# Attention and a gated feed-forward layer in one kernel: idle matrix products in the opening, edge loads on ScalarE's queue, additions for a reduction, and a table of priorities for the planned order

## The chip, the cores and the metric

The kernel runs on one core of a Trainium2 chip. The metric is the device time of one execution in microseconds (us). A time of "before" is the median of three runs; the profile is of one further execution, whose own time differs a little from that median and is given beside it below. Engines are called as in the profile: PE (TensorE, matrix products; PEld are its weight loads), DVE (VectorE), ACT (ScalarE), POOL (GpSimd) and SP (SyncE, which only issues transfers here). ACT and POOL issue transfers too.

## What is computed

The reference, cut to what matters:

```
B, H, S, D = 8, 8, 576, 64;  factor = 4
q_d, k_d, v_d = means of q, k, v over groups of 4 positions        # 144 rows
out_d  = softmax(q_d k_d^T / 8) v_d,  repeated 4 times along S     # coarse attention
local  = softmax(q k^T / 8, only |i - j| < 4) v                    # a band of 7 keys
x      = out_d + local, as 4608 rows of 512
xn     = x / sqrt(mean(x^2) + 1e-6) * rms_g
out    = (silu(xn w_gate) * (xn w_val)) w_out                      # 512 -> 1536 -> 512
```

## The kernel before

**The work.** The 4608 rows go through the feed-forward layer (`Forward`) in 18 chunks of 256. For each chunk, and for each of the 12 blocks of 128 hidden columns (f = 0 to 11), PE makes a gate part and a value part (line 1259, 12 products of 128x256 each) and, one pair of blocks later, the second layer (line 1296, 6 products of 128x512 each). Each fp32 operand is split into a high and a low part, so that three products of the fast type replace one of full precision: `xh`, `xl` for the rows, two tiles for each weight. The twelve blocks use three groups of weights, f = 0 to 3, 4 to 7 and 8 to 11.

**What must come before a chunk.** Chunk 0 and chunk 1 get their rows from `Early`: band attention on PE for two units of 128 rows each (units 0 and 1 for chunk 0, units 2 and 3 for chunk 1). A unit has four `score` steps (lines 1048 and 1050: a mask product of `one_sb` with `near_sb`, then the keys against `q`), maxima on DVE (line 1063), exponentials on ACT (line 1074), transposes (line 1108), the products with the values (line 1133), and the addition of the coarse result with a spreading matrix (line 1139). All other chunks get their rows from `Attention`, which works on DVE and ACT. The coarse attention (`Coarse`, lines 498, 526 and 540 on PE) comes in 32 items; the four of batch 0 belong to the opening, and their sums over four positions are made in the kernel by `OpeningSums`: `load_qk` fetches four parts, `add` (line 406) sums them on DVE with one reduction for each half, and `order` (line 402) copies the queries of the half to a tile `hs` on ACT, from which `score` takes them.

**The edges.** `Early.load_values` loads the 128 value rows of a unit (line 1028), and then, with eight small transfers of 2 KB (line 1036), the rows on its two sides into a tile of the pool `kv`, which POOL has cleared. Four units make 32 of these, and all are issued by SP.

**The weights.** They come as 64-bit words and are decoded in 20 pieces: the raw words are fetched by SP (line 249) into one of a few raw places, then POOL (line 264), ACT (line 254), DVE (line 271), ACT (line 278) and DVE (lines 283 and 285) make the high and the low tile. A raw place is free for the next piece when the last of these steps is done.

**What sets the order.** For the opening (all of the work until the third chunk is under way), a planner (`Plan`) writes the order of every engine by hand. Each `task` has an engine, a cost, a due time and what it waits for; the planner runs its own clock, and among the tasks that could start on an engine at about the same time takes the one with the smallest due time. Every engine executes its list in that order. After the opening, a loop writes the chunks in turn, and a scheduler sets the order.

A transfer from SP or ACT raises one of eight semaphores, given out in turn over both queues in the order in which the planner writes the transfers; an instruction that issues a transfer first waits until the transfer that had its semaphore before has landed.

Of the kernel before, what the change touches and what calls it, by code (L numbers as in the profile page):

```python
# [8 lines left out]
FP32 = mybir.dt.float32  # L9
# [5 lines left out]
ALU = mybir.AluOpType  # L15
# [23 lines left out]
EDGE = 2 * FAC  # L39
SPREAD = 13 * GRP  # L40
# [6 lines left out]
ON_TENSOR = 2  # L47
# [3 lines left out]
NEAR = 0.15  # L51
MB = 3.1
LAND = 2.0
ISSUE = 0.9

# [19 lines left out]
class Plan:  # L75


    def __init__(self, bufs):
        self.tasks, self.bufs = [], bufs
        self.order = {r: [] for r in bufs}  # L80
# [47 lines left out]
    def run(self, until=1e9):  # L128
        free, ready = self.free, self.ready
        while self.left:  # L130
            best = None
            for e, tasks in ready.items():
                found = []
                for t in tasks:
                    at = self.room(t) if t.allocs else 0.0
                    if at is not None:
                        floor = free["DMA"] - 3.0 if t.dma else 0.0
                        found.append((max(free[e], t.at, at, floor), t))
                if not found:
                    continue  # L140
                first = min(s for s, _ in found)
                pick = min(
                    ((next(o for o in t.options if o[0] == e)[2], t.n, s, t) for s, t in found if s <= first + NEAR),
                    key=lambda x: x[:2],
                )
                if best is None or pick[2] < best[0]:
                    best = (pick[2], e, pick[3])
            assert best, [t.fn for tasks in ready.values() for t in tasks][:40]
            s, e, t = best
# [3 lines left out]
            t.start = s  # L153
            free[e] = s + cost
# [19 lines left out]
def attn_moe_kernel(  # L174
# [34 lines left out]
    near_sb = const.tile([P, FAC * (NEAR_K + 1)], BF16, name="near_sb")  # L209

# [156 lines left out]
    class OpeningSums:  # L367


        def __init__(self, b, half):  # L370
# [5 lines left out]
            add = task("DVE", 2.5, self.add, at, [self.got], allocs=[self.qk_buf])  # L376
            self.q_got = task("ACT", 1.1, self.order, at - 1, [self.got], allocs=[self.q_buf])
# [26 lines left out]
        def add(self):  # L404
            self.qk = glob.tile([P, 2, 2, SD], FP32, name="qk")
            nc.vector.tensor_reduce(
                out=self.qk.rearrange("p t h n -> p (t h n)"),
                in_=self.raw_qk.rearrange("p j x -> p x j"), axis=AX.X, op=ALU.add,
            )

        def add_v(self, j, engine):
            if j == 1:
# [3 lines left out]
                out=vs, in0=self.raw_v[:, 0] if j == 1 else vs, in1=self.raw_v[:, j], op=ALU.add,  # L416
            )
# [3 lines left out]
    class Coarse:  # L421
# [28 lines left out]
        def plan(self, at, after=()):  # L450
# [12 lines left out]
            scores = task("PE", 0.75, self.scores, at, [*sm.ready_qk, *after], allocs=[*s, m, z], uses=[sm.qk_buf])  # L463
# [5 lines left out]
            for par in range(2):  # L469
                exps.append(task(  # L470
                    "ACT", 0.45, lambda par=par: self.powers(par), at, [scale], allocs=[a[par]], uses=[s[par], m, z],
                ))
            for par in range(2):
                turn = task("PE", 0.6, lambda par=par: self.turn(par), at - TAIL, [exps[par]], allocs=[t[par]], uses=[a[par]])
# [4 lines left out]
            values = self.valued = task("PE", 1.3, self.values, at - TAIL, [*copies, *sm.ready_vs], allocs=[o], uses=[*a, sm.vs_buf])  # L479
# [6 lines left out]
            stored[b, hp] = task("ACT", 0.06, self.store, at, [scaled], uses=[og], lag=2.2)  # L486
            return self

        def scores(self):
# [3 lines left out]
            self.s = [self.pool.tile([HALF, 2, SD], FP32, name=self.tag) for _ in range(2)]  # L493
            qs, ks = self.sums.qk[:, 0], self.sums.qk[:, 1]
# [27 lines left out]
        def turn(self, par):  # L522
            tp = self.t[par] = self.pool.tile([HALF, 2, SD], FP32, name=self.tag)
            for kc in range(2):
# [10 lines left out]
        def values(self):  # L535
            op = self.o = self.pool.tile([HALF, 2, 2, D], FP32, name=self.tag)
            for par, at in enumerate(self.a):
# [102 lines left out]
    class Attention:  # L640
# [55 lines left out]
        def plan(self, newton="POOL"):  # L696
# [7 lines left out]
            for n, jp in enumerate(jps):  # L704
                k_bufs[jp] = buf("kv"), buf("q_t")
                loaded[jp] = task(
                    "SP", 0.15, lambda jp=jp: self.load_score(*jp), T - 88 + 7 * n, allocs=k_bufs[jp],
# [20 lines left out]
            for n, jp in enumerate(jps):  # L728
                v_bufs[jp] = buf("kv")
                v_loaded[jp] = task(  # L730
                    "SP", 0.1, lambda jp=jp: self.load_value(*jp), T - 55 + 7 * n, allocs=[v_bufs[jp]],
# [774 lines left out]
```

## Time and profile before

| | |
|---|---|
| median of three runs | 1131.25 us (1128.24 to 1132.88) |
| profiled execution: its own time | 1137.31 us |
| profiled execution: span from first to last instruction | 1135.5 us |
| mean granted TensorE clock | 0.989 |
| PE busy, share of the span | 1083.9 us, 95% |
| DVE / ACT / POOL busy | 79% / 53% / 13% |
| lines 1259 and 1296, share of the chain that ended last | 50% and 25% |

How to read the lines below. A row of windows has the stretch in us, its length, then for PE, PEld, DVE, ACT and POOL the busy time with the count of instructions in brackets, the granted TensorE clock (1.00 is full speed), the busy share of the DMA engines, and GB/s. A row of the timeline has the start in us, the length, the engine, the line, the operation with out<-in, the shape and the count (a row merges equal neighbours); in square brackets stands how long the engine was idle before, and what ended that. SPq, ACTq and POOLq are the issuing of transfers. A row of waits has who waited for whom, the sum in us, how many times, and the longest.

### The profile page before, as it was taken

The numbers are of one execution on the slowest core, as the hardware profiler recorded it, in microseconds if no ns is written. First come the engines' busy times: TensorE is split into PE (matmuls) and PEld (weight loads), VectorE is DVE, ScalarE is ACT, GpSimd is POOL, SyncE is SP. The second block draws the span as 40 slices with busy tenths as digits, with TensorE's granted clock in tenths as the row PEclk, the third lists the DMA queues.
The fourth block names the chain that finished last, engine by engine and source line by source line (L and its number), as shares of the span: only waits on it lengthen the run. The fifth ranks groups of instructions, "written<-read, shape, count | busy, mean of one in ns | idle before, by whom it ended". The sixth has DMA issues, their size and how long they took to land.

```text
span 1135.5 us, 21446 instructions
## 1 busy us (share of the span) xinstructions
PE 1083.9 (95%) x7878; PEld 987.3 (87%) x7878; DVE 900.8 (79%) x1519; ACT 597.8 (53%) x2033; POOL 142.2 (13%) x178
## 2 busy tenths in 40 slices
PE   4699969989999999999999999999999999999997
PEld 3567869869999999999999999999999999999997
DVE  5365987869997979797979797979797989887321
ACT  3465547455646555555555555555555473736111
POOL 4242313332111010101010101010000000000000
PEclk9999989989999999999999999999999999999999
DMA  6755644636264344434343435343131313220000
GB/s 161 272 209 142 179 121 110 127 85 151 67 154 91 109 95 120 85 109 94 109 96 105 99 95 109 103 102 98 43 99 43 103 45 101 69 58 19 1 20 19
DMA packets 79619, 114.07 MB, mean 100 GB/s; under 512 B 32666, under 2 KB 41114, under 8 KB 79514
## 3 DMA queue, kind: packets, MB, share of 16 engines
q1 hardware_dynamic: 50026, 89.52, 25.8%
q0 software_dynamic: 10080, 18.59, 10.5%
q10 hardware_dynamic: 19408, 4.60, 1.9%
q8 instruction: 62, 1.02, 0.4%
q14 instruction: 43, 0.35, 0.1%
HBM read 100.86 MB, written 11.80 MB: 99 GB/s over the span
## 4 chain that ended last, share of the span: by engine, by line
PE 88%; DMA 5%; DVE 2%; ACT 2%; SPq 1%; issue 1%; POOL 0%; ACTq 0%; DVEq 0%; POOLq 0%
PE ps_h L1259 50%; PE ps_o L1296 25%; PE ps_a L540 3%; PE ps_a L498 2%; PE ps_a L526 2%; PE ps_a L926 1%; DMA wo<-in_w_val_dram 1%; PE ps_o L1133 1%; SPq L1036 1%; PE ps_h L1050 1%; DMA w<-in_v_pad_dram 1%; DMA w<-in_v_sum_dram 1%; PE ps_a L1133 1%; DMA q_t<-in_q_band_dram 1%; PE ps_a L1108 0%
## 5 line engine op out<-in xcount | busy, mean ns | idle before, releaser
L1259 PE MATMUL ps_h<-xh,w 128*128 128x256 f32 x3456 | 635.5, 281 | 10.7 <-ACT w L278 6.4
L1259 PEld LDWEIGHTS ps_h<-xh,w 128*128 128x128 f32 x3456 | 540.3, 189 | 22.7 <-ACT w L278 6.8
L1259 PE MATMUL ps_h<-xl,w 128*128 128x256 f32 x1728 | 483.5, 280 | 0.0
L1296 PE MATMUL ps_o<-wo,hs 128*128 128x512 f32 x1296 | 333.5, 399 | 1.7 <-POOL hs L1283 1.6
L1259 PEld LDWEIGHTS ps_h<-xl,w 128*128 128x128 f32 x1728 | 327.2, 189 | 6.5 <-issue 1.7
L857 ACT ACTIVATE prod<-kv,sc 128x64 f32<-128x64 f32 x1024 | 263.7, 407 | 30.4 <-DVE sc L848 19.8
L1296 PEld LDWEIGHTS ps_o<-wo,hs 128*128 128x128 f32 x1296 | 233.4, 189 | 46.4 <-POOL hs L1283 2.7
L874 DVE TENSOR_REDUCE x_t<-prod 128x128 f32<-128x896 f32 x128 | 135.0, 1078 | 47.4 <-PE ps_a L926 41.3
L1266 ACT ACTIVATE sil<-ps_h 128x512 f32<-128x512 f32 x108 | 64.5, 597 | 168.3 <-PE ps_h L1259 159.7
L1280 ACT ACTIVATE hs<-sil 128x512 fp32r<-128x512 f32 x108 | 68.2, 631 | 155.0 <-DVE sil L1274 134.2
L811 DVE TENSOR_TENSOR prod<-q_t,kv 128x896 f32<-128x896 f32 x128 | 140.0, 1099 | 0.5
L815 DVE TENSOR_REDUCE sc<-prod 128x14 f32<-128x896 f32 x128 | 136.7, 1076 | 0.5
L1269 DVE SCALAR_TENSOR_TENSOR sil<-sil,ps_h 128x512 f32<-128x512 f32 x108 | 73.5, 681 | 50.1 <-ACT sil L1266 49.8
L864 DVE TENSOR_TENSOR prod<-sc,kv 128x384 f32<-128x384 f32 (+1 forms) x128 | 103.6, 865 | 0.2
L1274 DVE SCALAR_TENSOR_TENSOR sil<-sil,ps_h 128x512 f32<-128x512 f32 x108 | 74.4, 690 | 30.5 <-PE ps_h L1259 30.3
L356 POOL DMA_DIRECT2D qk<-in_qk_sum_dram x42 | 37.7, 899 | 419.1 <-DMA qk<-in_qk_sum_dram 320.2
L1283 DVE TENSOR_TENSOR hs<-sil,hs 128x512 fp32r<-128x512 f32 x100 | 68.7, 687 | 18.9 <-ACT hs L1280 18.7
L897 ACT ACTIVATE up_t<-x_t 128x128 f32<-128x128 f32 x128 | 39.3, 307 | 44.0 <-DVE x_t L887 39.3
L517 ACT ACTIVATE a_g<-ps_a,m_g 72x144 f32<-72x144 f32 x128 | 46.4, 370 | 15.1 <-DVE m_e L1067 8.3
L605 ACT COPY a_g<-ps_a 72x288 f32<-72x288 f32 x63 | 22.8, 400 | 45.5 <-PE ps_a L526 45.3
L356 POOL DMA_DIRECT2D vs<-in_v_sum_dram x42 | 38.5, 916 | 53.3 <-DMA vs<-in_v_sum_dram 46.4
L540 PEld LDWEIGHTS ps_a<-vs,a_g 72*72 72x72 f32 x512 | 41.8, 159 | 1.3 <-ACT w L1074 0.5
(142 smaller groups left out, 806.9 us busy)
## 6 DMA issues: line engine op xcount, KB each, us to landing
kv<-in_k_pad_dram SPq DMA_DIRECT2D x56, 320.0 KB
kv<-in_v_pad_dram SPq DMA_DIRECT2D x56, 320.0 KB
qk<-in_qk_sum_dram POOLq DMA_DIRECT2D x42, 288.0 KB, 4.5
out_dram<-o_sb SPq DMA_DIRECT2D x96, 72.0 KB
q_t<-in_q_band_dram SPq DMA_DIRECT2D x170, 36.0 KB
vs<-in_v_sum_dram POOLq DMA_DIRECT2D x42, 144.0 KB, 4.4
w<-in_w_gate_dram SPq DMA_DIRECT2D x8, 512.0 KB
w<-in_w_val_dram SPq DMA_DIRECT2D x8, 512.0 KB
```

What stands on the lines that cost most here:

```text
L356: nc.gpsimd.dma_start(out=t, in_=(qk_sum, v_sum)[i][self.b, j, :, self.half], accum_op=ALU.add)
L540: nc.tensor.matmul(out=op[:, par, c], lhsT=at[:, kc, c * HALF:(c + 1) * HALF], rhs=self.sums.vs[:, 2 * (self.hp % 2) + par, kc], start=(kc ...
L811: nc.vector.tensor_tensor(out=pr, in0=bcast(q[:, s0:s0 + 2], 2, NO), in1=window(k, s0), op=ALU.mult)
L815: nc.vector.tensor_reduce(out=self.sc[:, j, par, s0:s0 + 2], in_=self.pr[i], axis=AX.X, op=ALU.add,)
L857: nc.scalar.activation(out=self.pr[i][:, o, s], in_=self.v[j, par][:, s0 + s + o], func=AF.Copy, scale=p[:, s, o:o + 1],)
L864: (nc.vector if engine == "DVE" else nc.gpsimd).tensor_tensor(out=self.pr[i][:, a:b], in0=bcast(p[:, :, a:b].rearrange("p s o -> p o s"), ...
L874: nc.vector.tensor_reduce(out=self.x[j][:, s0:s0 + 2, par], in_=pr.rearrange("p o s d -> p s d o"), axis=AX.X, op=ALU.add,)
L1259: nc.tensor.matmul(out=p[n][:, i], lhsT=wi[:, k], rhs=xi[:, k], start=(m == 0), stop=(m == 3 * KT - 1),)
L1269: nc.vector.scalar_tensor_tensor(out=self.sil[n], in0=self.sil[n], scalar=1.0, in1=self.g[n], op0=ALU.add, op1=ALU.mult,)
L1274: nc.vector.scalar_tensor_tensor(out=self.sil[n], in0=self.sil[n], scalar=0.5, in1=self.v[n], op0=ALU.mult, op1=ALU.mult,)
L1283: (nc.gpsimd if engine == "POOL" else nc.vector).tensor_tensor(out=self.hs[n][:, 1], in0=self.sil[n], in1=self.hs[n][:, 0], op=ALU.subtract,)
L1296: nc.tensor.matmul(out=self.o[j], lhsT=lhs[:, cols], rhs=rhs, start=(f == 0 and m == 0), stop=(f == NF - 1 and m == 2),)
```

## The change

- **Idle products.** A new function `heat` is called at the head of most PE steps of the opening. Where the planner's clock has PE idle ahead of the step, it writes products of a tile `zero_sb` (zeros in bf16) with `one_sb` into the output tile of the step, before the step's own products: 0.75 of the planned idle time, if that share is over 0.6 us. In the built program there are 60 of them: 35 of 256 columns ahead of the first `score`, 8 and 5 of 256 ahead of two transposes of the first coarse item, 8 of 512 ahead of the first product of chunk 0, and 4 of 512 in its second layer.
- **Edges.** The 32 small transfers become a task of their own, `load_edges`, issued by ACT. `load_values` keeps the one transfer of a unit.
- **Sums.** `add` becomes three additions for each half in place of one reduction.
- **Order.** A table `RANK` of one number for each task replaces the due times in the planner's choice (the diff shows its first line), and many costs are set anew.
- Small loads (`min_sb`, `g_sb`, `same_sb`) move from ACT's queue to POOL's, as a task; `one_sb` is made before `near_sb`.

```
+RANK = [
+    -2106, -457, -688, -997, -888, 97, 78, 175, 272, 77, -600, -444, 165, 52, 117, 74, 342, 176, 333, 142, 778,
...
         options = [(engine, cost, due)] if isinstance(engine, str) else list(engine)
+        if RANK:
+            by = RANK[len(self.tasks)] / 10 - options[0][2]
+            options = [(e, c, d + by) for e, c, d in options]
...
             t.start = s
+            self.idle = s - max(known, WARM_AT) if e == "PE" else 0.0
...
-            add = task("DVE", 2.5, self.add, at, [self.got], allocs=[self.qk_buf])
-            self.q_got = task("ACT", 1.1, self.order, at - 1, [self.got], allocs=[self.q_buf])
+            add = self.got
+            for j in range(1, FAC):
+                add = task(
+                    "DVE", 0.72, lambda j=j: self.add(j), at, [add], allocs=[self.qk_buf] if j == 1 else [], uses=[self.qk_buf],
+                )
+            self.q_got = task("ACT", 1.95, self.order, at - 1, [self.got], allocs=[self.q_buf])
...
-            nc.vector.tensor_reduce(
-                out=self.qk.rearrange("p t h n -> p (t h n)"),
-                in_=self.raw_qk.rearrange("p j x -> p x j"), axis=AX.X, op=ALU.add,
+            nc.vector.tensor_tensor(
+                out=qk, in0=self.raw_qk[:, 0] if j == 1 else qk, in1=self.raw_qk[:, j], op=ALU.add,
             )
...
+    def heat(out, fresh=True):
+
+        n, plan.idle = plan.idle * WARM_SHARE, 0.0
+        cols = 1
+        for d in out.shape[1:]:
+            cols *= d
+        if len(out.shape) > 2:
+            out = out.rearrange({3: "p a b -> p (a b)", 4: "p a b c -> p (a b c)"}[len(out.shape)])
+        cols = min(cols, 4 * P) // P * P
+        for _ in range(int(n * 2400 / cols) if n > WARM_LEAST and made else 0):
+            nc.tensor.matmul(
+                out=out[:, :cols], lhsT=one_sb[:, :out.shape[0]], rhs=bcast(zero_sb, 1, cols // zero_sb.shape[1]), start=fresh, stop=fresh,
+                skip_group_check=not fresh,
             )
...
-                v_got = task("SP", 0.9, lambda u=u: self.load_values(u), -90 + 12 * u, [clear], uses=[ve], dma=0.5 * MB)
+                v_got = task("SP", 0.4, lambda u=u: self.load_values(u), -90 + 12 * u, dma=0.5 * MB)
+                e_got = task("ACT", 2.8, lambda u=u: self.load_edges(u), -60, [clear], uses=[ve], lag=2.5)
...
-                nc.sync.dma_start(out=self.ve[u][h * EDGE:(h + 1) * EDGE, h * D:(h + 1) * D], in_=src)
+                nc.scalar.dma_start(out=self.ve[u][h * EDGE:(h + 1) * EDGE, h * D:(h + 1) * D], in_=src)
...
+    def load_small():
+        nc.gpsimd.memset(min_sb, 3e38)
...
+    small = task("POOL", 6.5, load_small, -40, not_before=2.5, lag=3.0)
+    one_got = task("POOL", 0.6, make_one, -70, not_before=4.5)
     near_got += [
-        task("POOL", 2.0, make_near, -60, not_before=2.5, allocs=[buf("sil"), buf("sil")]),
+        task("POOL", 1.5, make_near, -60, [one_got], allocs=[buf("sil"), buf("sil")]),
```

Where it moves the order. The first place is ACT's list at the start of the program. In before (`hs` is the tile of `order`; `w_1` names are raw tiles of the opening):

```order
L1361 DMA ident_sb<-in_ident_dram 128x128
L1365 DMA min_sb<-in_band_min_dram 4x28 x4
L1366 DMA g_sb<-in_rms_g_dram 128x4
L1367 DMA same_sb<-in_same_tok_dram 128x128
L402 ACT_TABLE_LOAD
L402 COPY hs<-w_1_102 128x1024
L402 COPY hs<-w_1_106 128x1024
```

And with the change:

```order
L1456 DMA ident_sb<-in_ident_dram 128x128
L1459 ACT_TABLE_LOAD
L1459 ACTIVATE zero_sb<-zero_sb 128x16
L1123 DMA kv<-in_v_pad_dram 8x1x64 x8
L1123 DMA kv<-in_v_pad_dram 8x64 x8
L1123 DMA kv<-in_v_pad_dram 8x1x64 x16
L463 COPY hs<-w_1_98 128x1024
L463 COPY hs<-w_1_110 128x1024
```

The 32 edge transfers now stand ahead of the two copies to `hs`; in before only six small transfers did.

The second place is SP's list, from its 14th transfer on, with the semaphores that each waits for (DMAHW0 to DMAHW7 are the eight of the transfers; `w_2` and `wo_2` are raw places of weights):

```order
L306 DMA o_sb<-in_w_out_dram 128x1024 [waits DMAHW3_49]
L306 DMA wo_2_343<-in_w_out_dram 128x1024 [waits DMAHW5_49]
L306 DMA wo_2_343<-in_w_out_dram 128x1024 [waits DMAHW7_49]
L306 DMA w_2_146<-in_w_gate_dram 128x1024 [waits DMAHW1_49]
L306 DMA w_2_146<-in_w_val_dram 128x1024 [waits DMAHW3_49]
```

And ACT's list with the change, from the 18th of the 32 edge transfers to the 23rd:

```order
L1123 DMA kv<-in_v_pad_dram 8x1x64 [waits DMAHW4_49]
L1123 DMA kv<-in_v_pad_dram 8x1x64 [waits DMAHW5_49]
L1123 DMA kv<-in_v_pad_dram 8x1x64 [waits DMAHW6_49]
L1123 DMA kv<-in_v_pad_dram 8x1x64 [waits DMAHW7_49]
L1123 DMA kv<-in_v_pad_dram 8x1x64 [waits DMAHW0_49]
L1123 DMA kv<-in_v_pad_dram 8x1x64 [waits DMAHW1_49]
```

Up to here SP's transfers have had DMAHW1, 3, 5 and 7, and ACT's the other four; from here on the edges go through all eight, so that the 19th waits for SP's first transfer to `wo_2_343`, the 21st for the second, and the 23rd for the gate words to `w_2_146`, SP's 17th transfer.

The third place is PE's list at its start (`ps_h` and `ps_a` are output tiles, `w_1` names raw tiles of the opening, `a_g` belongs to the coarse softmax). In before, the last `score` step ahead of the first coarse item, and that item's start:

```order
L1048 LDWEIGHTS one_sb
L1048 MATMUL ps_h<-near_sb,one_sb 128x272
L1050 MATMUL ps_h<-w_1_102,hs 128x136 x2
L498 MATMUL ps_a<-qk 72x144 x4
L526 MATMUL ps_a<-ident_sb,a_g 72x72 x8
```

With the change, where the four coarse products and the 35 idle products have gone before (the last idle one is the second row):

```order
L493 LDWEIGHTS one_sb
L493 MATMUL ps_h<-zero_sb,one_sb 128x256
L1136 LDWEIGHTS one_sb
L1136 MATMUL ps_h<-near_sb,one_sb 128x272
L1138 MATMUL ps_h<-w_1_98,hs 128x136 x2
```

The coarse scores, which need only the sums, now come first; the first `score` still needs `hs`, and everything after it on PE stands behind it.

More of the change, by code (lines that the diff above doesn't have):

```diff
@@ L39 @@
 EDGE = 2 * FAC
+ON_TENSOR = 2
 SPREAD = 13 * GRP
@@ L54 @@
 ISSUE = 0.9
+RANK = [
[46 rows of a table added]
+]
 class Buf:
@@ L137, in run @@
                         floor = free["DMA"] - 3.0 if t.dma else 0.0
-                        found.append((max(free[e], t.at, at, floor), t))
+                        found.append((max(free[e], t.at, at, floor), t, max(free[e], at)))
                 if not found:
                     continue
-                first = min(s for s, _ in found)
+                first = min(s for s, _, _ in found)
                 pick = min(
-                    ((next(o for o in t.options if o[0] == e)[2], t.n, s, t) for s, t in found if s <= first + NEAR),
+                    ((next(o for o in t.options if o[0] == e)[2], t.n, s, t, k) for s, t, k in found if s <= first + NEAR),
                     key=lambda x: x[:2],
@@ L462, in plan @@
                 whole_og["buf"] = og
-            scores = task("PE", 0.75, self.scores, at, [*sm.ready_qk, *after], allocs=[*s, m, z], uses=[sm.qk_buf])
+            scores = task("PE", 0.7, self.scores, at, [*sm.ready_qk, *after], allocs=[*s, m, z], uses=[sm.qk_buf])
             peaks = [
@@ L1343, in decode @@
             fetched.append(got)
-        bits = task("POOL", (0.93, 1.75)[m - 1], lambda: last_bits("POOL"), at, [got], uses=[raw])
+        bits = task("POOL", (0.75, 1.35)[m - 1], lambda: last_bits("POOL"), at, [got], uses=[raw])
         if fg == 0:
@@ L1362, in attn_moe_kernel, with make_one @@
     near_got, spread_sb = [], []
-    nc.gpsimd.memset(min_sb, 3e38)
-    for e, at, side in ((0, 0, 0), (1, P - KT, 1), (2, P // 2 - KT, 1), (2, P // 2, 0)):
-        nc.scalar.dma_start(out=min_sb[at:at + KT, e], in_=band_min[(P - KT) * side:(P - KT) * side + KT, side])
-    nc.scalar.dma_start(out=g_sb, in_=rms_g)
-    nc.scalar.dma_start(out=same_sb, in_=same_tok)
+    nc.vector.memset(zero_sb, -1e4)
+    nc.scalar.activation(out=zero_sb, in_=zero_sb, func=AF.Exp)
     used.update({"a": [], "b": [], "x": []})
+    def make_one():
+        nc.gpsimd.tensor_scalar(out=one_sb, in0=ident_sb, scalar1=2.0 ** 33, scalar2=None, op0=ALU.mult)
+        made.append(one_sb)
     def make_near():
@@ L1394, in attn_moe_kernel @@
         Coarse(*it).plan(12.0 + 4.0 * n)
+    def load_small():
+        nc.gpsimd.memset(min_sb, 3e38)
+        for e, at, side in ((0, 0, 0), (1, P - KT, 1), (2, P // 2 - KT, 1), (2, P // 2, 0)):
+            nc.gpsimd.dma_start(out=min_sb[at:at + KT, e], in_=band_min[(P - KT) * side:(P - KT) * side + KT, side])
+        nc.gpsimd.dma_start(out=g_sb, in_=rms_g)
+        nc.gpsimd.dma_start(out=same_sb, in_=same_tok)
+    small = task("POOL", 6.5, load_small, -40, not_before=2.5, lag=3.0)
+    one_got = task("POOL", 0.6, make_one, -70, not_before=4.5)
     near_got += [
-        task("POOL", 2.0, make_near, -60, not_before=2.5, allocs=[buf("sil"), buf("sil")]),
+        task("POOL", 1.5, make_near, -60, [one_got], allocs=[buf("sil"), buf("sil")]),
         task("POOL", 0.8, make_spread, -50, not_before=2.5),
@@ L1409, in attn_moe_kernel @@
         decode(n)
-    atts[1].turns[0].after += fetched
+    for t in fetched:
+        atts[1].turns[0].after.append(t)
     for c in range(FIRST):
```

66 lines of the change are left out of this document (43 added, 23 removed), and 45 rows, old and new, of the table RANK.

## The prediction

> **What bounds the kernel now.** I read the busy times of the page first, and then the windows between the places where the granted clock changes.
>
> ```profile
> PE 1083.9 (95%) x7878; PEld 987.3 (87%) x7878; DVE 900.8 (79%) x1519; ACT 597.8 (53%) x2033; POOL 142.2 (13%) x178
> ```
>
> ```profile
> 0.00:42.00 42.00, 16.98 (x83) 12.61 (x84) 18.00 (x29) 13.47 (x41) 13.15 (x27) 1.00 0.59 171
> 42.00:108.80 66.80, 62.68 (x249) 44.96 (x247) 38.80 (x75) 39.45 (x99) 24.56 (x18) 1.00 0.65 219
> 108.80:151.80 43.00, 37.96 (x262) 33.44 (x262) 40.52 (x55) 22.53 (x36) 15.19 (x14) 1.00 0.72 193
> 151.80:162.10 10.30, 4.96 (x22) 4.54 (x22) 8.59 (x10) 4.62 (x7) 1.09 (x1) 0.50 0.12 36
> 162.10:237.20 75.10, 70.23 (x568) 64.15 (x567) 55.29 (x99) 42.44 (x156) 23.45 (x27) 1.00 0.49 113
> 237.20:247.40 10.20, 9.08 (x37) 6.46 (x36) 5.32 (x11) 3.63 (x13) 4.92 (x15) 0.50 0.14 27
> 247.40:1129.40 882.00, 882.00 (x6668) 821.15 (x6666) 734.26 (x1245) 471.09 (x1684) 59.80 (x78) 1.00 0.34 84
> ```
>
> PE is busy for 95% of the span, and in the last 882 us without a gap, so no reordering of DVE or ACT shortens that part. What the change can win lies in the first 247 us, and of it I make two parts. From 108.8 to 247.4 PE has 5.04 + 5.34 + 4.87 + 1.12 = 16.4 us without work, and in the two rows with the clock at 0.50 it does 4.96 + 9.08 us of work at half rate, of which (14.04)/2 = 7.0 us is loss: together **23.4 us**. The rest is the time until chunk 0 runs without a break, 108.8 us.
>
> The clock column reads 1.00 in the first two rows too. PE's timeline says otherwise:
>
> ```profile
> 89.98 0.63 PE L1259 MATMUL ps_h<-xh,w 128*128 128x256 f32 x2
> 90.41 0.41 PE L1259 MATMUL ps_h<-xl,w 128*128 128x256 f32 x1
> ...
> 108.80 0.39 PE L1259 MATMUL ps_h<-xh,w 128*128 128x256 f32 x1 [1.41 <-DVE sil L1269]
> ...
> 109.14 0.39 PE L1259 MATMUL ps_h<-xh,w 128*128 128x256 f32 x2
> 109.37 0.28 PE L1259 MATMUL ps_h<-xl,w 128*128 128x256 f32 x1
> ```
>
> Two products and the start of the next are 90.41 - 89.98 = 0.43 us apart, 0.213 us each; at 109 us it is 0.23 us, 0.114 each. So the whole of the early work ran at half rate, and the 1.00 stands for a clock of which there is no record yet. That PE is busy isn't enough to raise it:
>
> ```profile
> 60.00:80.00 20.00, 19.93 (x73) 13.26 (x74) 12.32 (x21) 14.62 (x39) 9.28 (x5) 1.00 0.70 244
> 236.32 0.39 PE L904 MATMUL ps_a<-ss,same_sb 128*128 128x8 f32 x2 [4.20 <-ACT up_t L897]
> ```
>
> From 60 to 80 us PE has 19.93 of 20 us of work (transposes, products of 64 rows or 64 columns) and stays slow, since the products at 90 us are slow. And one gap of 4.20 us, ended at 236.32, was followed by the half clock from 237.2, for 10.2 us.
>
> **Edges and the order of ACT.** This is the part on which the forecast rests. In before SP issued the edges:
>
> ```profile
> 2.35 9.99 SPq L1036 DMA_DIRECT2D kv<-in_v_pad_dram  x8
> ...
> 13.73 9.41 SPq L1036 DMA_DIRECT2D kv<-in_v_pad_dram  x8
> ...
> 29.48 5.24 SPq L1036 DMA_DIRECT2D kv<-in_v_pad_dram  x8
> ...
> 34.77 0.40 SPq L249 DMA_DIRECT2D w<-in_w_gate_dram  x1
> ```
>
> ```profile
> SPq L1036 <- DMA w<-in_qk_sum_dram: 3.3, 2, 2.8
> ...
> SPq L1036 <- DMA w<-in_v_sum_dram: 3.0, 2, 2.5
> ```
>
> Eight of them took 5.24 to 9.99 us of SP, and the waits say for what: not for their own data, but for large transfers (`qk_sum`, `v_sum`) that had their semaphore before. The weights could start only at 34.77. With the change they start behind `qk_sum` and `v_sum`, and it is ACT that issues the edges, ahead of both copies to `hs`. In before the copies came here:
>
> ```profile
> 1.22 2.06 ACTq L1365 DMA_DIRECT2D min_sb<-in_band_min_dram  x4
> 5.45 0.36 ACTq L1366 DMA_DIRECT2D g_sb<-in_rms_g_dram  x1
> ...
> 8.20 3.84 ACT L402 COPY hs<-w 128x1024 f32<-128x1024 f32 x2
> ```
>
> By the order, the 19th, 21st and 23rd edges wait for SP's 15th, 16th and 17th transfers. When does the 17th land? It and those before it carry two `qk_sum` (128x2304 fp32, 1.18 MB each), two `v_sum` (0.59), one unit of values (0.26), and twelve weight pieces (128x1024 words, 0.524 each): 10.1 MB.
>
> ```profile
> 4.00:6.00 2.00, 0.00 (x0) 0.00 (x0) 0.00 (x0) 0.00 (x0) 1.72 (x5) 1.00 1.04 410
> 16.00:18.00 2.00, 0.00 (x0) 0.00 (x0) 2.00 (x3) 0.00 (x0) 0.00 (x0) 1.00 0.98 208
> 42.00:44.00 2.00, 2.00 (x18) 2.00 (x17) 0.30 (x2) 1.61 (x2) 1.12 (x1) 1.00 1.02 414
> ```
>
> With all engines of the DMA full the trace moves 0.41 MB/us, so 24.6 us; `v_sum` (72 rows) moves at 0.21, which adds 1.18/0.21 - 1.18/0.41 = 2.7 us; with the start and a landing of 2 us each it is 31 us. Nine more edges follow, at 0.3 us each: the copies start at **35 us** (30 to 38) instead of 8.2. Only the four first coarse products of PE can go before that. The nearest row on the other side is that of the six small loads above, 0.36 us each when nothing is waited for: 32 x 0.36 = 11.5 us, and the copies at 14 (rival C).
>
> The Trainium skill ("DMA: Bandwidth & Descriptors", "Queues, rings and completion order") has the engines serve the queues in turn, a packet at a time, so that a small transfer on ACT's own queue need not stand behind SP's large ones. By it alone the copies would start as in rival C. The waits of line 1036 on `qk_sum` above disagree: issuing, not moving, was held.
>
> **When chunk 0 runs unbroken (X).** The work of PE up to there:
>
> ```profile
> L1048 PE MATMUL ps_h<-near_sb,one_sb 128*128 128x272 bf16 x16 | 6.7, 421 | 7.7 <-POOL one_sb L1382 7.4 <-ACT wo L1074 0.3
> L498 PE MATMUL ps_a<-qk 64*72 64x144 f32 x32 | 8.0, 458 | 0.0
> L1259 PE MATMUL ps_h<-xh,w 128*128 128x256 f32 x16 | 5.7, 435 | 0.0
> ...
> L1259 PE MATMUL ps_h<-xl,w 128*128 128x256 f32 x8 | 3.3, 416 | 0.0
> ```
>
> From the windows 16.98 + 62.68 = 79.7 us. Off it go the 16 + 8 products of chunk 0 that before had done by then (24 x 0.213 = 5.1), one of the four coarse scores and one of the 16 masks, which now stand ahead of the wait (8.0/4 + 6.7/16 = 2.4). On it come the 8 + 5 idle products of 256 columns (13 x 0.213 = 2.8): 75.0 us. PE was busy for 62.68/66.80 = 93.8% of the second window and for 99.7% of the densest one; at their mean, 96.7%, it takes 77.6 us. The first copy takes 3.84/2 = 1.9, and the 8 idle products of 512 columns ahead of chunk 0, at half rate, 8 x 0.43 = 3.4. X = 35 + 1.9 + 77.6 + 3.4 = **117.9 us**, 9.1 later than in before.
>
> Is PE really the bound there? ACT has 13.47 + 39.45 = 52.9 us of work before 108.8, so it could be through at 88, and DVE with 56.8, less the reductions below, at about 92 even with some waiting. The long wait of ACT for weights goes, since the weights are there:
>
> ```profile
> ACT w L254 <- DMA w<-in_w_val_dram: 10.2, 1, 10.2
> ```
>
> It is worth nothing by itself, because PE had work beside it.
>
> **Idle products.** The 35 first ones lie between the first coarse scores and the first `score`, at some 10 to 17 us; PE waits for `hs` then, so 35 x 0.213 = 7.5 us costs nothing. They can raise the clock, but some 18 us without work follow until 37, and the trace needed only 4.20 us for a fall. The 13 later ones are 2.8 us, at most; the work after them is that of the row from 60 to 80 us, which did not raise the clock. So I take PE as slow until chunk 0. The 8 of 512 columns are dense, and chunk 0 starts at the full clock or a few us later; the 24 products that now come after X cost 24 x 0.114 = 2.7 us.
>
> The Trainium skill ("TensorE: Matmul & The Clock Gate", "Part 1: The HAM clock gate") gives the same verdict on the first 35: the clock rises after a busy window of 3413 ns and falls after idle ones. The 4.20 us gap and the 10.2 us at half rate agree; its busy window taken as any work is rival B.
>
> **Sums by additions.** Rows of DVE's timeline:
>
> ```profile
> 6.54 4.21 DVE L406 TENSOR_REDUCE qk<-w 128x576 f32<-128x2304 f32 x1 [6.54 <-DMA w<-in_qk_sum_dram]
> ...
> 19.89 1.41 DVE L415 TENSOR_TENSOR vs<-vs,w 72x512 f32<-72x512 f32 x2 [1.29 <-POOL vs L415]
> ```
>
> Three additions at about 0.7 (of 512 columns; 576 here) in place of 4.21 us, twice: 2 x 2.1 us less on DVE. All of it lies ahead of the wait for `hs`, so it counts nothing; if that wait were gone, it is 2 us at the first coarse item. The small loads on POOL have the same cover.
>
> **After X.** The weights of the first two groups are there early. The third group was late in before:
>
> ```profile
> 149.49 0.39 PE L1259 MATMUL ps_h<-xh,w 128*128 128x256 f32 x1 [2.36 <-ACT w L278]
> ...
> 156.01 0.58 PE L1259 MATMUL ps_h<-xh,w 128*128 128x256 f32 x1 [4.08 <-ACT w L278]
> ```
>
> ```profile
> 152.28 1.10 ACT L254 ACTIVATE wo<-wo 128x1024 f32<-128x1024 f32 x1 [2.84 <-DMA wo<-in_w_val_dram]
> ```
>
> PE asked for it 149.5 - 108.8 = 40.7 us after X, and so would at 159 now. The last piece needs a raw place, a transfer and 3.7 us from its first step on ACT to the product (152.28 to 156.01). Opening work and decoding are over earlier relative to X, but the last four loads of the group stand behind two groups of loads of `kv` and `q_t`. I leave **s = 5 us** of stalls after X, between none and the 12.9 of the third and fourth windows (5.04 + 5.34 + 4.96/2); the four idle products in chunk 0's second layer (0.9 us) and a late rise of the clock are in it.
>
> **Sum.** 9.1 + 2.7 - 23.4 + 5 = -6.6 us. The profiled execution took 1137.3 (span 1135.5), 6.1 above the median; on the median it is 1131.25 - 6.6 = **1125** us, 0.6% less. About 0.5%, 5.7 us, is what a measurement of this kernel can tell from no change.
>
> **The rivals.**
>
> A, the sum above: 0.58. Its own range: t of the copies 30 to 38 gives -5 to +3, s -5 to +8: 1117 to 1134.
>
> B, PE is fast from the first score on. For it: the 35 products raise the clock, the 13 at some 38 us may do it again. Against it: the row from 60 to 80 us. PE's 75 us halve, and DVE is the bound: from 37 us 48.4 us of work (18.00 + 38.80 less 8.4), at 80% busy 60: X = 97. As PE then asks for the third group at 138, s is 10: -11.8 + 2.7 - 23.4 + 10 = -22.5, **1109**. 0.13.
>
> C, the change does not hold ACT: the semaphores are free in time, and the copies start at 14. X = 97, and -24 with s = 8: **1107**. 0.09. Against it stand SP's own rows, where eight edges took 10 us.
>
> D, slower: the third group of weights comes as late as before and later, because its last pairs stand behind two groups of loads of line 593 and 799, where one stood before.
>
> ```profile
> 135.02 0.58 SPq L593 DMA_DIRECT2D kv<-in_k_pad_dram  x1
> 135.65 4.03 SPq L799 DMA_DIRECT2D q_t<-in_q_band_dram  x5
> 139.79 0.35 SPq L249 DMA_DIRECT2D wo<-in_w_gate_dram  x1
> ```
>
> A group held SP for 139.79 - 135.02 = 4.8 us; stalls 12.9 + 4.8 and the second cold stretch kept, 10.2 - 9.08/2 = 5.7: s = 23, +12: **1143**. It decides from s = 11.6 on, and is slower by over 0.5% from 17. 0.20: the loads of the group are issued earlier relative to X, which speaks against it.
>
> **How the numbers follow.** Half of A lies below 1125.6, so faster has 0.27 of A, B and C: 0.49; the same has 0.28 of A and 0.02 of D: 0.30; slower the rest, 0.21. The range goes from a little below C, 1102, to the lower part of D, 1139; outside are most of D and a little of B and C.
>
> **What would show it.** Right: ACT's last edge issued at 33 to 37 us, waiting for weight transfers; both copies to `hs` behind it; PE without work from about 17 to 37 us; products of line 1259 0.114 us apart only from about X = 118; SP's first weight at under 5 us. Right on the second part: less than 10 us without work on PE from X to 250, and at most one row at 0.50. Wrong: copies before 20 us (C), the transposes of 60 to 80 us in half their time (B), PE waiting for the third group for over 12 us (D), or a wait of DVE or ACT that bounds the early work though the weights are there.

## The result and the profile after

The changed kernel takes **1140.86 us** (median of 6 runs, 1138.39 to 1143.87), the kernel before 1131.06 in the same comparison (6 runs): a ratio of 1.009, with a 95% interval of 1.007 to 1.011. It is slower by 9.8 us. The forecast was 1125, 6.6 less than before, in a range of 1102 to 1139: wrong in sign and outside the range. The profiled execution took 1140.74 us, at the median.

Its windows, cut where PE gets `hs`, where chunk 0 begins to run, and where the clock changes:

```profile
0.00:42.42 42.42, 6.37 (x45) 4.78 (x45) 8.37 (x13) 3.50 (x4) 23.38 (x38) 0.73 0.75 255
42.42:121.70 79.28, 73.89 (x318) 52.26 (x318) 54.42 (x111) 50.09 (x139) 17.63 (x16) 0.52 0.51 148
121.70:159.30 37.60, 35.40 (x271) 32.02 (x269) 32.71 (x47) 19.34 (x35) 11.45 (x11) 1.00 0.72 191
159.30:166.20 6.90, 5.43 (x24) 4.73 (x25) 6.18 (x5) 4.24 (x6) 5.72 (x4) 0.51 0.25 100
166.20:213.90 47.70, 46.45 (x379) 42.95 (x377) 39.32 (x67) 27.10 (x87) 13.78 (x15) 1.00 0.41 95
213.90:220.80 6.90, 6.12 (x31) 5.64 (x32) 3.76 (x6) 4.93 (x19) 2.85 (x4) 0.51 0.64 104
220.80:1132.00 911.20, 909.46 (x6874) 844.82 (x6874) 755.68 (x1288) 485.85 (x1737) 71.03 (x99) 1.00 0.34 85
```

In the first 42 us PE has 6.4 us of work, where before had 17. From 42.4 to 121.7 it is 93% busy at a clock of 0.52. Chunk 0 starts at 121.7, against 108.8 for its unbroken products in before.

What held PE stands in ACT's timeline, in pieces that begin at 14.37, 22.27, 31.12 and 37.78 us (each shows the edges of a few us, waits between them included), and in the row for all 32 edge transfers (shortest, median and longest issue in ns, first and last start):

```profile
14.37 3.29 ACTq L1123 DMA_DIRECT2D kv<-in_v_pad_dram  x3
...
22.27 2.92 ACTq L1123 DMA_DIRECT2D kv<-in_v_pad_dram  x3
...
31.12 3.26 ACTq L1123 DMA_DIRECT2D kv<-in_v_pad_dram  x5
...
37.78 2.60 ACTq L1123 DMA_DIRECT2D kv<-in_v_pad_dram  x4
```

```profile
40.42 1.94 ACT L463 COPY hs<-w 128x1024 f32<-128x1024 f32 x1 [37.68 <-DMA kv<-in_v_pad_dram]
```

```profile
L1123 ACTq DMA_DIRECT2D kv<-in_v_pad_dram x32: 277/620/1266, 1.3 to 39.8; - x32
```

The first 18 edges went out by 25.2 us. The 19th was issued at 31.12; from it on, the 14 that were left followed each other by 0.66 us with no wait between them. The copies start at 40.42. PE's timeline shows what that meant:

```profile
10.35 5.08 PE L493 MATMUL ps_h<-zero_sb,one_sb 128*128 128x256 bf16 x35
...
42.42 1.28 PE L1138 MATMUL ps_h<-w,hs 64*128 64x136 f32 x4 [26.86 <-ACT hs L463]
...
118.64 3.46 PE L493 MATMUL ps_h<-zero_sb,one_sb 128*128 128x512 bf16 x8
121.70 0.52 PE L1353 MATMUL ps_h<-xh,w 128*128 128x256 f32 x1
122.06 0.28 PE L1353 MATMUL ps_h<-xl,w 128*128 128x256 f32 x1
...
160.77 2.19 PE L622 MATMUL ps_a<-vs,a_g 72*72 72x64 f32 x16 [3.27 <-ACT a_g L687]
...
214.68 2.08 PE L1391 MATMUL ps_o<-wo,hs 128*128 128x512 f32 x4 [2.03 <-POOL hs L1377]
```

The 35 idle products are followed by a wait of 26.86 us; the eight ahead of chunk 0 are followed at once by products at the full rate. Behind them no wait for weights is left (in before the same products, on line 1259, had four of them), but two others, of 3.27 and 2.03 us, each with a stretch at half clock beside it.

### The profile page after: what moved, and what is told of

Read it like the earlier page. It is cut to its first block, busy times and chain, and to the rows that moved or that the text cites. A ratio compares the mean times of both kernels' runs of the same rounds, so it can differ in the third digit from the quotient of the medians.

```text
span 1138.9 us, 21554 instructions
## 1 busy us (share of the span) xinstructions
PE 1084.1 (95%) x7938; PEld 987.7 (87%) x7938; DVE 900.4 (79%) x1534; ACT 596.2 (52%) x2024; POOL 145.8 (13%) x184
## 4 chain that ended last, share of the span: by engine, by line
PE 89%; DVE 2%; DMA 1%; ACT 1%; POOL 1%; issue 1%; SPq 0%; ACTq 0%; POOLq 0%; DVEq 0%
PE ps_h L1353 51%; PE ps_o L1391 26%; PE ps_a L622 3%; PE ps_a L578 2%; PE ps_a L1009 1%; PE ps_a L607 1%; PE ps_o L1224 1%; PE ps_a L1224 1%; DMA wo<-in_w_val_dram 1%; PE ps_h L1138 0%; PE ps_a L1197 0%; PE ps_a L1231 0%; PE ps_o L1231 0%; DMA qk<-in_qk_sum_dram 0%; PE ps_h L493 0%
## 5 line engine op out<-in xcount | busy, mean ns | idle before, releaser
L939 ACT ACTIVATE prod<-kv,sc 128x64 f32<-128x64 f32 x1024 | 264.1, 408 | 32.4 <-DVE sc L930 19.1
L1377 DVE TENSOR_TENSOR hs<-sil,hs 128x512 fp32r<-128x512 f32 x99 | 67.8, 685 | 19.6 <-ACT hs L1374 19.5
L622 PE MATMUL ps_a<-vs,a_g 72*72 72x64 f32 x512 | 43.2, 243 | 3.3 <-ACT a_g L687 3.3
```

The costliest lines, as they stand in the source:

```text
L622: nc.tensor.matmul(out=op[:, par, c], lhsT=at[:, kc, c * HALF:(c + 1) * HALF], rhs=self.sums.vs[:, 2 * (self.hp % 2) + par, kc], start=(kc ...
L939: nc.scalar.activation(out=self.pr[i][:, o, s], in_=self.v[j, par][:, s0 + s + o], func=AF.Copy, scale=p[:, s, o:o + 1],)
```

## The experiments

Twelve runs were made, two of them of the kernel before unchanged. In them **theory 1** is: 32 small issues hold whatever list they stand in; with the change that is ACT's, the copies to `hs` and all of the early work stand behind it, and this is what made the kernel slower. **Theory 2**, its rival, puts the start of chunk 0 down to something else (the table's order, PE at half rate). Theories 3 to 6 are on the idle products. "Start of chunk 0" is its first product in the profile; for before and kernels made from it, the unbroken products.

**The edges written later.** ACT issues the edges of a unit behind the unit's exponentials; the plan is otherwise that of the change.

```
-  e_got = task("ACT", 2.8, lambda u=u: self.load_edges(u), -60, [clear], ...)
+  e_got = task("ACT", 2.8, lambda: None, -60, [clear], ...)
   def invert(self, u):
       ...
+      self.load_edges(u)
```

> The changed kernel with the same plan, but the 32 edge transfers are written on ACT where the exponentials of their unit are done, not at the head of its list. Theory 1 (ACT's list is held by the edges until 40.4 us, and everything behind the copies to hs with it): copies at 8 to 10 us, chunk 0 unbroken from 91 to 100 us instead of 121.7, and the time 1112 to 1123 us. Theory 2 (the order from the table, with PE at half rate, sets the start of chunk 0; the copies would have been early enough): chunk 0 from 115 to 122, time 1136 to 1141.

1124.68 us (10 runs, 1112.9 to 1128.5), ratio 0.9915 (0.9881 to 0.995): 16 us below the changed kernel. From its ACT and PE timelines:

```profile
6.39 2.01 ACT L463 COPY hs<-w 128x1024 f32<-128x1024 f32 x1 [3.67 <-DMA w<-in_qk_sum_dram]
9.97 2.00 ACT L463 COPY hs<-w 128x1024 f32<-128x1024 f32 x1 [1.57 <-DMA w<-in_qk_sum_dram]
```

```profile
104.10 0.47 PE L1354 MATMUL ps_h<-xh,w 128*128 128x256 f32 x1
```

The copies now wait for their data and for nothing else. Chunk 0 starts 17.6 us earlier, somewhat later than expected (91 to 100), and the median is 1.7 us above the expected range. The order from the table was kept, so theory 2 falls.

**The edges in four transfers.** Same plan, same place in ACT's list, but one transfer per unit. It comes from an array that is laid out beforehand with the zeros between the heads, so that POOL needn't clear the tile.

```
-  for h in range(H): ...
-      nc.scalar.dma_start(out=self.ve[u][h * EDGE:(h + 1) * EDGE, h * D:(h + 1) * D], in_=src)
+  nc.scalar.dma_start(out=self.ve[u], in_=v_edge[u])
```

> The changed kernel with the edges of a unit as one transfer of 128 KB from an array that is laid out with the zeros in it: 4 issues on ACT at the same place in place of 32, and no clearing on POOL. Theory 1: copies at 8 to 12 us, chunk 0 unbroken from 88 to 98 us, time 1108 to 1120; and if the issuing itself is dear on ACT (0.65 us each, 32 of them 21 us), 3 us or more below the run with the edges written later. Theory 2: as there, 1136 to 1141.

1121.77 us (5 runs), ratio 0.9912 (0.9875 to 0.9948). ACT's and PE's timelines:

```profile
2.66 1.42 ACTq L1117 DMA_DIRECT2D kv<-in_v_edge_dram  x2
7.20 2.00 ACT L464 COPY hs<-w 128x1024 f32<-128x1024 f32 x1 [4.46 <-DMA w<-in_qk_sum_dram]
```

```profile
94.19 0.47 PE L1347 MATMUL ps_h<-xh,w 128*128 128x256 f32 x1
```

Chunk 0 starts at 94.2, 27.5 us earlier than with the change, within the expected range; the time fell by 19 in the median. It is 1.8 us above what was expected, and its interval overlaps that of the run before. In the two profiled executions the 9.9 us by which chunk 0 starts earlier than there came through in full (1118.51 against 1128.47 us), but the one is almost the fastest of its five and the other the slowest of its ten; the medians differ by 2.9, where 3 or more was the sign for issues that are dear wherever they stand. So these runs show that the issues were dear at the head of the list; what they cost behind the exponentials stays open, though ACT's own work still stood behind them there for 7.2, 4.6 and 2.7 us.

**One part alone, from the other side.** The kernel before, only with ACT as the issuer:

```
-  nc.sync.dma_start(out=self.ve[u][h * EDGE:(h + 1) * EDGE, ...], in_=src)
+  nc.scalar.dma_start(out=self.ve[u][h * EDGE:(h + 1) * EDGE, ...], in_=src)
```

> The kernel before with one part of the change alone: the edge transfers are issued by ACT instead of SP, where they were written (eight ahead of the copies to hs, 24 right behind them); order, costs, sums as before. Theory 1 (they hold ACT's list as they held SP's, and the exponentials stand behind them): the first exponential on ACT at 35 to 42 us, the weights in SP's list from 5 to 12 us, chunk 0 unbroken from 108 to 116, time 1131 to 1139 us. Theory 2 (moving them off SP is the gain, and ACT has room for them): chunk 0 before 101 and 1121 to 1126, as in the run of before with four transfers.

1149.86 us, ratio 1.0168 (1.0127 to 1.0209): slower by 19 us, further than theory 1 had it; the unbroken products start at 120.03 (108 to 116 expected; 108.8 in before). PE's waits up to 60 us, and ACT's timeline:

```profile
PE ps_a L526 <- ACT a_g L517: 18.3, 1, 18.3
PE ps_h L1050 <- ACT hs L402: 16.5, 1, 16.5
```

```profile
7.42 13.68 ACTq L1036 DMA_DIRECT2D kv<-in_v_pad_dram  x8
...
25.61 20.34 ACTq L1036 DMA_DIRECT2D kv<-in_v_pad_dram  x21
46.05 0.38 ACT L517 ACTIVATE a_g<-ps_a,m_g 72x144 f32<-72x144 f32 x1 [19.77 <-DMA kv<-in_v_pad_dram]
```

Eight edges ahead of the copies and the rest behind them make two waits of PE, 34.8 us together, where the changed kernel has the one of 26.86. The first exponential is at 46.05, behind the last edge. The edges on ACT alone, with no table and no idle products, make the kernel slower.

**And the reverse.** The kernel before with the four larger transfers, still on SP.

> The kernel before, with the edges of a unit as one transfer of 128 KB from an array that is laid out with the zeros in it, issued by SP: 4 issues in place of 32, no clearing, all else as it was. Theory 1 (32 small issues hold whatever list they stand in; in before that was SP's, and the weights behind them): SP's first weight at 8 to 12 us instead of 34.8, ACT's wait of 10.2 us for it gone, chunk 0 unbroken from 96 to 101 instead of 108.8, time 1119 to 1125 us. Theory 2 (in before the edges cost nothing, the early work has its own bound): 1129 to 1133.

1124.61 us, ratio 0.9917 (0.9896 to 0.9938), as expected; the unbroken products start at 95.52 instead of 108.8. Two details were not as expected, by SP's timeline and ACT's waits:

```profile
13.13 5.25 SPq L1032 DMA_DIRECT2D kv<-in_v_edge_dram  x1
...
19.98 0.58 SPq L250 DMA_DIRECT2D w<-in_w_gate_dram  x1
```

```profile
ACT w L1070 <- DMA w<-in_w_gate_dram: 9.6, 1, 9.6
```

The first weight goes out at 19.98, not at 8 to 12, since a single issue still took up to 5.25 us of SP; what held it the profile does not say. So ACT's wait for weights only moved. But what stood behind it on PE shrank. In before, then here:

```profile
41.24 1.12 PE L1108 MATMUL ps_a<-ident_sb,w 128*128 128x128 f32 x4 [10.03 <-ACT a_g L605]
```

```profile
32.82 0.38 PE L1044 MATMUL ps_h<-near_sb,one_sb 128*128 128x272 bf16 x1 [4.28 <-ACT w L1070]
```

In before ACT's copy on line 605 stood right behind its wait of 10.2 us for weights, and PE had nothing to do for 10.03 us; here it is 4.28, and 0.51 later on. Part of the other 8 us is that PE ran at the full rate for some of the early work here (16 products of line 1133 took 3.67 us each time in before; of the three such groups here two took 2.00). The edges were what cost in before as well. This kernel, with nothing else of the change, has the ratio of the change with four transfers (0.9917 and 0.9912): by the medians all the rest of the change together is worth nothing that these runs can tell. The two profiled executions leave it open, since the part behind chunk 0's start takes 1029.3 us here and 1022.2 there.

**The sums.** One reduction again in place of three additions, in the changed kernel.

> The changed kernel with one reduction for each half in place of the three additions, all else as changed. Theory 1 (the sums lie ahead of PE's wait for hs): no difference, 1138 to 1143 us, ratio to before 1.006 to 1.012; first coarse scores on PE some 2 us later than 9.2. Theory 2 (they are part of what sets the start of chunk 0): 1142 to 1146.

1141.49 us, ratio 1.0089 (1.0056 to 1.0121): no difference from the change. The first coarse scores came at 10.86 instead of 9.19 us, 1.7 later, and PE then waited 25.0 us for `hs` instead of 26.9.

**The table.** The changed kernel with an empty table, so that due times set the order.

```
-RANK = [ ... ]
+RANK = []
```

> The changed kernel without the table: the due times of the tasks set the plan's order, all else as changed. Theory 1 (the edges at the head of ACT's list, where the due times put them too, set the start of chunk 0): copies to hs at 38 to 42 us, chunk 0 unbroken from 115 us or later, and the time at 1138 or more; the table then only moves what comes after. Theory 2 (the table is what makes it slow): copies as late, but chunk 0 before 112, and 1125 to 1133.

1161.07 us, ratio 1.0237 (1.0211 to 1.0264). The copies are late here too (42.58), as theory 1 had it, but chunk 0 starts at 107.5, which neither theory gave together with such a time. It is no clean test: the plan without the table believes PE idle far more often, and so writes 248 idle products instead of 60. The groups of idle products of the two kernels, first this one and then the changed one:

```profile
L446 PE MATMUL ps_a<-zero_sb,one_sb 128*72 128x256 bf16 (+1 forms) x192 | 25.7, 293 | 0.0
L446 PE MATMUL ps_o<-zero_sb,one_sb 128*128 128x512 bf16 x21 | 6.2, 433 | 0.0
L446 PE MATMUL ps_h<-zero_sb,one_sb 128*128 128x256 bf16 x35 | 5.2, 320 | 0.0
```

```profile
L493 PE MATMUL ps_h<-zero_sb,one_sb 128*128 128x256 bf16 (+1 forms) x43 | 8.5, 371 | 0.0
...
L493 PE MATMUL ps_a<-zero_sb,one_sb 128*72 128x256 bf16 x13 | 3.2, 422 | 0.0
...
L493 PE MATMUL ps_o<-zero_sb,one_sb 128*128 128x512 bf16 x4 | 1.0, 382 | 0.0
```

That is 37.1 us of idle products against 12.7; the 24.4 more exceed the 20.2 us between the two kernels. But they don't explain it alone: behind chunk 0's start there are 18.8 us of them against 1.0, and the rest of the program takes 1047.4 us there against 1017.2, 30.2 more. What the table is worth by itself stays open.

**No idle products.**

```
-WARM_SHARE = 0.75
+WARM_SHARE = 0.0
```

> The changed kernel without its 60 idle products, the plan unchanged. Theory 1 (the first 35 lie in a wait, the 13 in the first coarse item nearly so, and the 8 ahead of chunk 0 cost 3.1 us and bring the full clock at 121.7, without which some 3 us of chunk 0 run at half rate): 1138 to 1144, no difference. Theory 3 (the idle products are the loss: 3.3 us ahead of transposes, 3.1 ahead of chunk 0): 1133 to 1136. Theory 4 (they hold the clock up where it counts): 1146 or more.

1135.96 us (10 runs), ratio 1.004 (1.0012 to 1.0068), against 1.009 (1.007 to 1.011) for the change: the medians are 4.9 us apart, and the intervals just touch. This is the upper end of theory 3 (1133 to 1136) and below theory 1 (1138 to 1144). The 60 idle products probably cost some microseconds. PE's timeline without them:

```profile
118.84 0.58 PE L1353 MATMUL ps_h<-xh,w 128*128 128x256 f32 x1 [0.68 <-ACT xh L1272]
...
122.50 0.63 PE L1353 MATMUL ps_h<-xh,w 128*128 128x256 f32 x2
122.93 0.38 PE L1353 MATMUL ps_h<-xl,w 128*128 128x256 f32 x1
123.14 0.40 PE L1353 MATMUL ps_h<-xh,w 128*128 128x256 f32 x2
```

Chunk 0 starts 2.9 us earlier, at half rate, and reaches the full rate at 123.1, after 4.3 us of its own products (2.1 us lost). Real products raise the clock as well as idle ones do; the eight ahead of chunk 0 bought 2.1 us for 3.1.

**More idle products.** In the kernel with four transfers, idle products of at least 1024 columns are written ahead of every PE step up to chunk 0, planned idle time or not. (`stop` is filled by chunk 0's first product.)

```
-  for _ in range(int(n * 2400 / cols) if n > WARM_LEAST and made else 0):
+  for _ in range(max(int(n * 2400 / cols) if n > WARM_LEAST else 0, 0 if stop else 1024 // cols) if made else 0):
```

> The changed kernel with the edges in four transfers, and with idle products of at least 1024 columns in all ahead of every PE step up to the first product of chunk 0, whether or not the plan has PE idle there. There the clock was 0.50 from 23 to 88 us with PE busy. Theory 5 (enough idle products between the real ones hold the clock up): the early work at full rate, chunk 0 unbroken from 76 to 88 us instead of 94.2, time 1104 to 1115. Theory 6 (the clock falls all the same, and the products are added work, 0.85 us each step at half rate): chunk 0 from 110 or later, 1130 or more.

1114.62 us, ratio 0.9834 (0.9812 to 0.9855): the fastest kernel here, faster than before and than the change. The time is what theory 5 said; the way to it isn't. Windows of this kernel, and then of the one with four transfers alone:

```profile
23.00:36.00 13.00, 13.00 (x112) 10.31 (x111) 10.76 (x23) 10.45 (x31) 8.41 (x6) 0.91 1.01 383
36.00:90.00 54.00, 50.15 (x319) 33.97 (x318) 40.94 (x80) 32.88 (x91) 18.43 (x12) 0.94 0.60 185
```

```profile
23.00:36.00 13.00, 12.75 (x72) 9.98 (x71) 10.78 (x22) 10.62 (x32) 7.14 (x6) 0.51 1.02 381
36.00:88.00 52.00, 44.26 (x182) 31.12 (x180) 39.22 (x75) 30.29 (x86) 14.58 (x12) 0.50 0.59 190
```

The clock was held for most of the time, 0.91 and 0.94 in the mean instead of 0.51 and 0.50. But chunk 0 starts at 95.2, not at 76 to 88, and no earlier than without (94.2). The groups of PE up to there say why, again first with and then without:

```profile
L494 PE MATMUL ps_a<-zero_sb,one_sb 128*72 128x256 bf16 (+2 forms) x109 | 19.5, 303 | 0.7 <-ACT a_g L598 0.6
L1132 PE MATMUL ps_h<-w,hs 64*128 64x136 f32 x64 | 19.1, 429 | 0.0
L494 PE MATMUL ps_h<-zero_sb,one_sb 128*128 128x256 bf16 (+1 forms) x102 | 17.4, 315 | 3.1 <-ACT w L1156 3.1
L623 PE MATMUL ps_a<-vs,a_g 72*72 72x64 f32 x64 | 4.8, 227 | 0.0
```

```profile
L1132 PE MATMUL ps_h<-w,hs 64*128 64x136 f32 x64 | 20.4, 452 | 0.0
L623 PE MATMUL ps_a<-vs,a_g 72*72 72x64 f32 x64 | 8.7, 330 | 0.0
```

The largest group of the early work, the 64 products of the keys with `q`, takes 19.1 us at the full clock and 20.4 at half; only others, such as line 623, nearly halve. And the idle products took 36.9 us. Where the gain comes from is not settled. The medians are 7.2 us apart, the two profiled executions only 1.5 in span (1114.9 and 1116.4): the part behind chunk 0's start is 2.5 us shorter, and the rest of the 7.2 isn't in these profiles.

Half as many, 512 columns ahead of each step:

> As the run with four transfers and 1024 idle columns ahead of each step, with 512. Theory 5 (half as many still hold the clock, and each one less is time saved): chunk 0 unbroken from 82 to 90 us instead of 95.2, time 1102 to 1110. Theory 6 (512 are too few, the clock falls): chunk 0 from 98 on, and 1118 or more.

1119.85 us, ratio 0.9914 (0.9882 to 0.9946), no different from the kernel with four transfers. The clock was at half (0.50 to 0.52) from 23 to 78 us, and chunk 0 started at 105.7. This is theory 6, in its mechanism and in its time (1118 or more).

The 1024 columns in the changed kernel, its 32 edges at the head of ACT's list:

> The changed kernel, edges as changed, with idle products of at least 1024 columns ahead of every PE step up to chunk 0. Theory 5 (they hold the clock from the copies on): 75 us of early work at half rate become 38 and some 23 us of idle products, so chunk 0 unbroken from 104 to 111 instead of 121.7, time 1122 to 1131. Theory 6 (they help only where the copies come early, before the fall): chunk 0 from 130 on, 1148 or more.

1137.98 us (7 runs), ratio 1.0075 (1.005 to 1.01): no difference from the change. Chunk 0 starts at 118.8, between what the theories gave; the clock is back at the full rate at 49 us and, after a fall, from 73 on. With the copies at 40 us, the idle products gave back 3 us of the start of chunk 0 and no time that can be told from none.

**The kernel before, twice more.** Unchanged, for second and third profiles.

> The kernel before, unchanged, for a second profile of it. The prediction summed against a profiled execution of 1137.3 us, 6.1 above the median of 1131.25. Theory 1: that execution held a stretch at half clock that most do not have (its stretch from 237.2 to 247.4 us, worth 9.08/2 = 4.5 us of work, and the 4.2 us gap ahead of it); a second profile with a time near 1131 shows one stretch less or a shorter gap. Theory 2: the profiler adds the 6 us evenly; a second profile shows both stretches and both gaps again, at 1136 to 1138.

> The kernel before once more, for a profile of an execution of its usual time (20 of 26 runs lay at 1128 to 1134 us, 6 at 1137 to 1138.1). Theory 1: an execution near 1130 has one of the two stretches at half clock less, or a shorter one, than the profiled one of 1137.3. Theory 2: it has both, and another 6 us are missing elsewhere.

1131.80 us in ten runs (ratio 1.0003, 0.9977 to 1.0028), of which the profiled one took 1137.45; the single run of the other took 1137.84. Both profiles show the same two stretches at half clock, at the same places to within 0.6 us, and nearly the same gap ahead of the second (3.96 and 3.80 us, where the first profile had 4.20). So all three traces of before are of executions some 6 us above its median, and none is of a usual one. What a usual one lacks could not be seen. Both stretches again, at 1137.45, is what the first text names for theory 2, that the profiler adds the 6 us; but one more of the ten runs took 1137.32, and four of the 26 it was compared with took 1137 to 1138 (the second text counts all six under the 26), so it need not be the profiler.

## Why the prediction was wrong

**The mechanism of the edges was right, the price of what follows the wait was not.** The step put the landing of SP's 17th transfer at 31 us, as the end of the last wait, that of the 23rd edge. The last wait was that of the 19th edge, for the 15th transfer, and it ended at 31.12; that the times agree is partly luck. The 21st and the 23rd waited no more. "Nine more edges follow, at 0.3 us each: the copies start at 35 us (30 to 38)" failed: 14 edges were left, not nine, and they followed each other by 0.66 us, not 0.3. That is 9.3 us instead of 2.7, and the copies came at 40.4. (The step's own terms add up to 34.0, not 35.) The row for 0.66 was there: four groups of eight edges on SP, two of them in 5.24 us, 0.655 each, with no wait for another transfer in them. The prediction read these as waits, and took the price from single small loads; there too, the four of line 1365 in 2.06 us were 0.5 each, not 0.36. (0.3 us is what the eight edges of unit 0 take; those left in the list were of the other form, see the end.)

**Chunk 0** therefore started at 121.7 instead of 117.9. From the first product with `hs` to the idle products it took 118.64 - 42.42 = 76.2 us for a forecast of 77.6, at a clock of 0.52. It is close by two errors that cancel: PE had 70.8 us of work there, not 75.0, and 5.4 us without, not 2.6, all of it waits for ACT (DVE was busy for 19.5 of the 20 us from 60 to 80). That PE stays slow there (against rival B), that the edges hold ACT (against rival C), and that the first 35 idle products are lost, was right. So were the sums, which count nothing. Wrong was the reading that ACT's wait of 10.2 us for weights in before was worth nothing "because PE had work beside it": PE waited 10.03 us behind it, as the row at 41.24 above shows. The sum does not rest on it, but the worth of four transfers in before does.

**After chunk 0's start** "I leave s = 5 us of stalls" failed as a size. The windows give 2.20 + 1.47 + 1.25 + 0.78 + 1.74 = 7.4 us without work, (5.43 + 6.12)/2 = 5.8 lost at half clock, and 1.0 of idle products: 14.2. Rival D's place for it was wrong: the weights of the third group came in time. New waits took their place (line 622 for ACT, line 1391 for POOL), which I had not looked for: with a stall gone, I priced the next one by a share of the old and did not ask whose work is late next. From chunk 0's start to the end before took 1135.5 - 108.8 = 1026.7 us and the change 1138.9 - 121.7 = 1017.2, 9.5 less; forecast were 15.7. By these terms it would be 2.7 + 14.2 - 23.4 = -6.5; the other 3.0 us I could not place. Of the signs named for this part, less than 10 us without work came true (7.0 up to 250 us), and at most one row at half clock did not: there were two.

**The base.** Between the profiled executions the difference is 1140.74 - 1137.31 = +3.4, against -6.6 forecast: 3.8 of the miss is the start of chunk 0, 6.2 what came after it. The medians differ by +9.8, 6.4 more. "On the median it is 1131.25 - 6.6" failed there: the profiled execution of before lay 6 us above the median, as all three traced ones did, and that of the change lay at its median. The stalls of 23.4 us were read from an execution that took 6 us longer than the usual one. Whether the usual one lacks part of just these stalls was not shown.

**The idle products** were priced at 2.8 us for the 13 in the first coarse item, 3.4 for the eight ahead of chunk 0, 0.9 for the last four, and nothing for the first 35. Without all of them the median is 4.9 us lower, by intervals that touch, so this price was of the right size. The Trainium skill's rule ("TensorE: Matmul & The Clock Gate", "Part 1: The HAM clock gate") that a window of sustained work gives the full rate agrees with products that were dense: 3.1 us of idle products ahead of chunk 0, or 4.3 us of chunk 0's own. For the early work the trace decides against it, if any busy PE counts: from 100 to 118 us in the changed kernel PE was busy without a gap and stayed at half clock. What it is in the work that decides stays open: in the kernel before with four transfers, such work did reach the full rate, from about 63 to 72 us (the 2.00 us in place of 3.67 above).

```profile
100.00:118.00 18.00, 18.00 (x61) 12.46 (x61) 9.25 (x24) 7.07 (x22) 4.54 (x5) 0.50 0.64 147
```

The cause of the slowdown is shown from both sides: undoing only the place of the edges, or only their number (and with it the clearing on POOL), takes 16 and 19 us off, and moving only them to ACT in before adds 19. What was forecast as the gain behind chunk 0's start is less well understood.

## What to carry to other kernels

Small transfers cost their issuer: count them by the spacing of the same transfers, in the same form, in a row, and count what each waits for, before moving them to an engine whose own work stands behind them. Better than finding a queue for 32 transfers was making four of them. When a stall in the trace is to be removed, ask what comes second there, and check by how much the profiled execution stands off the median before its stalls are added up as a gain.

## What the runs showed of the hardware

- What an issue of 2 KB takes of ACT went by the form of the transfer, not by whether it had waited. In the changed kernel the eight edges of unit 0, whose rows lie next to each other (8x64 in the list of the change), took 0.28 to 0.33 us each; of the other 24 (8x1x64) the first took 1.27, the others 0.62 to 0.65, after a pause as well as directly behind another (then 0.66 from start to start). The kernel with the edges written later has three of unit 0 directly behind each other, at 0.30. One of each form in the changed kernel, both after a pause:

```profile
6.97 0.62 ACTq L1123 DMA_DIRECT2D kv<-in_v_pad_dram  x1
20.38 0.28 ACTq L1123 DMA_DIRECT2D kv<-in_v_pad_dram  x1
```

- The key products of 64x136 in fp32 hardly follow the clock: 429 ns each with 0.91 to 0.94 granted, 452 with 0.50; products of 72x64 went from 330 to 227.
- Idle bf16 products of 1024 columns ahead of each step held the granted clock at 0.91 and more in the mean through work that alone left it at 0.50, in the kernel with four transfers; it still fell to 0.50 from about 42 to 49 us, in and behind a wait of 3.12 us. 512 columns did not hold it.
- The granted clock can fall early in a gap. In the changed kernel, by windows of 0.25 us, it fell 1.9 us into the gap of 3.27 us and 1.3 us into the one of 2.03, with PE busy right up to each.
